# The first group's output products in the half-size scheme of the other groups, and the last store cut in two

## The chip, the cores and the metric

The kernel runs on one core of one Trainium2 chip. The metric is the device time of one execution in microseconds (us), as the median of several runs. Beside these, one execution was taken by the hardware profiler; the durations in the text come from that one.

## The reference

Two stages follow each other. The first is a gated linear recurrence over 768 steps for 4 batches x 8 heads of width 48; the second is a maxout layer on the 3072 resulting tokens of width 384.

```python
f = 1.0 / (1.0 + np.exp(-f_logit))
for t in range(S):                                   # S = 768
    state = f[:, :, t, :, None] * state + np.einsum('bhd,bhe->bhde', k[:, :, t], v[:, :, t])
    y[:, :, t] = np.einsum('bhd,bhde->bhe', q[:, :, t], state)
x = y.transpose(0, 2, 1, 3).reshape(3072, 384)
h = np.maximum(np.maximum(x @ w1, x @ w2), x @ w3)   # w1, w2, w3: 384 x 768
out = h @ w_out                                      # 768 x 384
```

## The kernel before

**Units and groups.** The recurrence is cut into 24 units: a unit is one chunk of 64 steps for two batches, 128 tokens. Four units make a group of 512 tokens, so there are six groups, numbered 0 to 5. As soon as a group's x is complete (xT, feature-major), the group's maxout products are queued, and the units of the next group run between them.

**How the order is set.** Everything is written out by hand in one order (no scheduler moves it), and each engine works through its own part of that order. The products of a group are a Python generator that issues a few matmuls and then yields what they cost; `fill(ns)` draws from it until that many nanoseconds of matmul work are issued. The main loop over units calls `fill` four times in a unit, with the lengths EARLY (units 4 to 7, 2360 ns) or PART (later ones), and issues between these calls the steps of the unit: the block of small matmuls on TensorE (`values`, `sums`, `pairs`, `finish`: lines 415, 433, 396, 504), the scans, transposes and products on VectorE and GpSimd (`scan`, `after`, `before`, `carry`: r L329, ends L339, kh L340, qh L351, state L357), the keys (`keys_by_blocks`, ks L382), and the loads of later units (L183 for f, k, q; L164 for v). SP issues nearly all DMAs, in the written order.

**Maxout without the first weight.** w2 and w3 are kept as differences to w1, so that x @ w1 can leave the maximum and be added at the end: `linear` (L788) computes w1 @ w_out once into w_nat, 18 products of 384 columns, copied out by ScalarE (L792). Then out = hm @ w_out + x @ w_nat, where hm is the maximum of x @ (w2 - w1), x @ (w3 - w1) and 0.

**Group 0** (`ffn_first`) does its products while the weights still arrive and are turned from float64 to fp32. Its outputs (`outputs`, L568) are plain: for each of its four units one bank, nine products of 384 columns (six with hm, three with x), and one copy to o on ScalarE (L572).

**Groups 1 to 5** save matmul work by a scheme of Strassen's kind: seven products of half size replace eight, at the price of sums and differences of the operands. It is used for the inputs (`inputs_by_pairs`, L884, whose weight sums are made by `mix_in`, L853, and whose sums of x are made by `sums_of_x`, L868) and for the outputs (`outputs_by_pairs`, L637, products of 192 columns). For the outputs GpSimd makes the sums of weights (`mix`, L592; `mix_x`, L600) and of hm (`sums_of_hm`, L608: four for each of three pairs of hm rows). Partial results are copied from the banks by ScalarE (L642, L692, L721) and added up by VectorE (L645) and GpSimd (L704) into o. In these groups the first 256 features of x go through the scheme along with hm, as one more pair.

**Rearranged weights.** `place` issues ten small DMAs that copy a weight matrix, with its rows in another order, from one place on the chip to another: w_in[1] to placed[0] and w_in[2] to placed[1] (L458, L465) for the inputs of groups 1 to 5, and w_nat to w_lin for their outputs. placed[2] is then free and holds the sums of `mix_in`; w_in[2] holds those of `mix`; w_in[1] holds the sums of hm.

**The last group** adds its last quarter of the outputs in two halves as the banks c and d are ready (L645), and stores it with one DMA on SP and one on ScalarE's queue (`store_part`, L744), each of 64 partitions x 2 x 192.

Of the kernel before, what the change touches and what calls it, by code (L numbers as in the profile page):

```python
# [9 lines left out]
FP32 = mybir.dt.float32  # L10
# [3 lines left out]
ALU = mybir.AluOpType  # L14
# [32 lines left out]
C = 64  # L47
# [8 lines left out]
def kernel(  # L56
# [12 lines left out]
    nc = tc.nc  # L69
# [8 lines left out]
    GRP = 4  # L78
# [11 lines left out]
    def fast():  # L90
        ctx = ExitStack()
        with ctx:
# [439 lines left out]
            def bank(in_tr=False):  # L532
                if in_tr:
                    return ps_tr.tile([128, TOK], FP32, name="tr")
                return ps_f.tile([128, TOK], FP32, name="p")
# [23 lines left out]
                    t0 = (2 * bp + a) * S + c * C  # L559
                    nc.sync.dma_start(out=out[t0:t0 + C, :], in_=o[a * C:(a + 1) * C, :])  # L560

            def outputs(hm, xT, i):
                p = bank()
                t = slice(i % 2 * UT, (i % 2 + 1) * UT)
                terms = [(hm[:, j, i * UT:(i + 1) * UT], w_out[:, j, :]) for j in range(NJ)]
                terms += [(by_halves(xT)[:, i // 2, k, t], w_nat[:, k, :]) for k in range(NK)]
                for n, (lhsT, rhs) in enumerate(terms):
                    nc.tensor.matmul(p[:, 0:DM], lhsT=lhsT, rhs=rhs, start=(n == 0), stop=(n == NJ + NK - 1))  # L568
                    if n % NK == NK - 1:
                        if n == NJ + NK - 1:  # L570
                            o = o_four[:, i]
                            nc.scalar.copy(o, p[:, 0:DM])  # L572
                            late.append((i, o))
                        yield NK * DM * COLUMN

            HJ, HD = NJ // 2, DM // 2  # L580
            corner = lambda k, n: w_out[:, k::2, n * HD:(n + 1) * HD]
            w_mix = [corner(0, 1)] + [w_in[2][:, :, n * HD:(n + 1) * HD] for n in range(4)]
            x_mix = [w_lin[:, 0, HD:]] + [w_mix[4][:, n] for n in range(2)] + [keep.tile([128, HD], FP32, name="mix")]
            s_mix = [w_in[1][:, n, :].rearrange("q (jj t) -> q jj t", jj=HJ) for n in range(NK)]
            s_last = keep.tile([128, HALF], FP32, name="s_last")
# [1 line left out]

            def mix(n):

                dst, x, y = ((w_mix[2], corner(1, 1), corner(0, 1)), (w_mix[0], corner(0, 1), corner(0, 0)),  # L590
                             (w_mix[1], corner(1, 1), w_mix[0]), (w_mix[3], corner(1, 0), w_mix[1]))[n]
                nc.gpsimd.tensor_tensor(dst, x, y, op=ALU.subtract)  # L592

            def mix_x(n):

# [14 lines left out]
            def sums_of_hm(hm, jj):  # L610
                sums_of_pair(hm[:, 2 * jj], hm[:, 2 * jj + 1], *(t[:, jj] for t in s_mix))
# [7 lines left out]
            def outputs_by_pairs(g, hm, xT):  # L619
                tile_of = lambda p, n: slice((2 * p + n) * UT, (2 * p + n + 1) * UT)  # L620
                half = lambda n: slice(n * HD, (n + 1) * HD)
                order = [*range(HJ - 1), HJ, HJ - 1]
                A = lambda k, n: lambda p: [(xT[:, k] if jj == HJ else hm[:, 2 * jj + k])[:, tile_of(p, n)] for jj in order]
                C = lambda k, n: [(w_lin[:, k] if jj == HJ else w_out[:, 2 * jj + k])[:, half(n)] for jj in order]
                T = lambda i: [x_mix[i] if jj == HJ else w_mix[i][:, jj] for jj in order]
                s1, s2, s4 = (lambda p, t=t, x=x: [(x if jj == HJ else t[:, jj])[:, p * UT:(p + 1) * UT] for jj in order]
                              for t, x in zip(s_mix, s_of_x(xT)))
                X = lambda n: lambda p: [xT[:, 2, tile_of(p, n)]]
                lin, lin_mix = [[w_lin[:, 2, half(n)]] for n in range(2)], [w_mix[4][:, 2]]
                partial = [w_nat[:, n, :] for n in range(NK)]  # L630
                last = g == NU // GRP - 1
                tight = g >= NU // GRP - 2
                begun = set()
# [10 lines left out]
                def add(out, b, n, at=slice(0, 2)):  # L644
                    nc.vector.tensor_tensor(out[:, at], pairs_of(b[:, 0:DM])[:, at], pairs_of(partial[n])[:, at], op=ALU.add)  # L645
# [11 lines left out]
                sums_of_x_pair(xT, 0)  # L657
                into(b, 0, X(0), lin[0])
                yield PLAIN
                into(b, 1, X(0), lin[0])  # L660
# [1 line left out]
                early, rest = slice(len(order) - 1), slice(len(order) - 1, None)  # L662
                for p in range(2):
                    into(a, p, A(0, 0), C(0, 0), early)
                    if p:
# [59 lines left out]
                into(c, 0, s4, C(1, 1))  # L725
                if last:
                    add(o_of(0, 1), c, 1, slice(0, 1))
                yield COST
                into(d, 1, s4, C(1, 1))
                if last:  # L730
                    add(o_of(0, 1), d, 1, slice(1, 2))
                    store_part(g, 0, 1, both)
                else:
                    add(o_of(0, 1), c, 1)
                    late.extend((g * GRP + i, o_four[:, i]) for i in (1, 3, 0, 2))
# [1 line left out]

            o_of = lambda n, c: o_four.rearrange("t (p n) c -> t n p c", p=2)[:, n, :, c * HD:(c + 1) * HD]

            def store_part(g, n, c, queues=one):  # L740

                for a in range(2):
                    t0 = (2 * n + a) * S + 2 * g * C
                    queues[a].dma_start(out=out[t0:t0 + 2 * C, c * HD:(c + 1) * HD].rearrange("(p r) c -> r p c", p=2),  # L744
                                        in_=o_of(n, c)[a * C:(a + 1) * C])

            late = []

# [49 lines left out]
            def ffn_first(xT):  # L798
                hm = new_hm()
                steps = [(j, slice(n * HALF, (n + 1) * HALF)) for n in range(2) for j in range(J_HALF)]  # L800
                steps += [(j, slice(0, TOK)) for j in range(J_HALF, NJ)]
                n_step = 0
                for j, t in steps:
                    w = t.stop - t.start
                    for i in (1, 2):
                        p = yield from product(xT, j, i, t)
                        if i == 1:
                            nc.scalar.copy(hm[:, j, t], p)
                        else:
                            nc.vector.scalar_tensor_tensor(hm[:, j, t], hm[:, j, t], 0.0, p, op0=ALU.max, op1=ALU.max)  # L810
                        round_to(ROUNDED[n_step])
                        load_weights(2, rounded[0] - 1)
                        yield (1 if w == TOK else NK) * w * COLUMN
                        n_step += 1
                        if n_step in TURNED:
                            yield from turn(TURNED[n_step])
                for a in range(NK):
                    if a < 2:
                        for n in range(2 * NK + 2):
                            place(placed[a].bitcast(FP32), w_in[a + 1], n)  # L820
                    for cost in linear(a):
                        round_to(rounded[0] + 1)
                        yield cost
                for n in range(2 * NK + 2):
                    place(w_lin, w_nat, n)
                made = iter([lambda n=n: mix_in(n) for n in range(4)] + [lambda: mix(0)])
                for i in range(GRP):
                    for n, cost in enumerate(outputs(hm, xT, i)):
                        if i or n:
                            next(made, lambda: None)()  # L830
                        if i == GRP - 1 and n == 1:
                            mix(1)
                            if 1 in packed:
                                sums_of_x(1)
                        if i == GRP - 1 and n == 2:
                            for k in range(2, 4):
                                mix(k)
                        yield cost

            w_two = [t.bitcast(FP32) for t in placed[0:2]]
            w_sum = [placed[2].bitcast(FP32)[:, n] for n in range(NK)]

            def mix_in(n):

# [141 lines left out]

            CHECKS = 2 * GRP + 2
            STEP = NK * HALF * COLUMN
            EARLY = 2360
            PART = (33 * TOK + 64 * HD) * COLUMN / (5 * GRP)


# [2 lines left out]
            with tc.manual_schedule():  # L999
# [77 lines left out]
                fill(2 * STEP)  # L1077
                for u in range(GRP, NU):
                    n = u + 1
                    part = EARLY if u < 2 * GRP else PART  # L1080
                    if n == BY_ROWS:
                        scan(n)
                    fill(part)
# [332 lines left out]
```

## Time and profile before

| what | value |
|---|---|
| median of 3 runs | 412.28 us (410.96 to 412.45) |
| the profiled execution | 408.62 us |
| its span, first to last instruction | 406.9 us |
| granted TensorE clock | 0.999 |
| busy: TensorE / VectorE / GpSimd / ScalarE | 391.8 / 293.8 / 246.1 / 180.7 us |
| group 0: `linear` on TensorE, first to last start | 76.2 to 89.8 us |
| group 0: outputs on TensorE, first start to last end | 90.1 to 117.7 us |
| group 1: outputs on TensorE | 152.9 to 177.1 us |
| last matmul's end, last add's end | 401.9, 402.3 us |

How to read the views: a line of the chain or of a timeline has the start, the length, the engine, the line of the kernel, what is done and how often (xN). PE is TensorE, PEld its weight loads, DVE VectorE, ACT ScalarE, POOL GpSimd, SP the engine that issues DMAs (SPq is its queue). An fp32 product of the program stands as two records. A bracket at a line's end is the idle time of the engine before it, and whose end closed it.

### The profile page before, as it was taken

The page shows a single profiled execution, that of the slowest core. Times are in us where ns is not written, and L with a number is a line of the kernel's source. Part 1 is how long each engine was busy: PE and PEld are TensorE (multiplying, and loading weights), DVE is VectorE, ACT ScalarE, POOL GpSimd, SP SyncE. Part 2 cuts the span into 40 slices and gives each one's busy share as a digit, 9 for nine tenths or more (in the row PEclk, how much of TensorE's full clock was granted, in tenths as well). Part 3 has the DMA queues.
Part 4 walks back from the last instruction along what each step waited for, and adds up shares of the span by engine and source line. Part 5 has one row for each costly group of instructions (what it writes and reads, how often), then busy time and mean ns, then how long its engine had stood idle before and what let it go on. Part 6 is the DMA issues. An engine that isn't in the chain of part 4 may idle for free.

```text
span 406.9 us, 11516 instructions
## 1 busy us (share of the span) xinstructions
PE 391.8 (96%) x4598; PEld 331.6 (81%) x4598; DVE 293.8 (72%) x569; ACT 180.7 (44%) x430; POOL 246.1 (60%) x270
## 2 busy tenths in 40 slices
PE   4988999999999999999999999999999999999995
PEld 4766765556678888998889988899988899988994
DVE  6997797997886999897998987998995450012500
ACT  2488787422224541435442344523354425576210
POOL 2189695843888797387486287667477850525700
PEclk9999999999999999999999999999999999999999
DMA  8989986776467776276645367734473003541012
GB/s 173 253 260 280 254 232 92 151 147 89 93 90 111 89 164 129 63 112 86 119 123 100 56 110 92 163 72 81 66 148 107 2 17 98 134 144 59 0 21 63
DMA packets 181562, 47.21 MB, mean 116 GB/s; under 512 B 160448, under 2 KB 179200, under 8 KB 181504
## 3 DMA queue, kind: packets, MB, share of 16 engines
q1 hardware_dynamic: 178032, 45.62, 54.5%
q10 hardware_dynamic: 3472, 0.81, 0.9%
q8 instruction: 37, 0.61, 0.6%
q14 instruction: 21, 0.17, 0.1%
HBM read 37.75 MB, written 4.72 MB: 104 GB/s over the span
## 4 chain that ended last, share of the span: by engine, by line
PE 82%; DVE 8%; issue 2%; SPq 2%; POOL 2%; ACT 1%; DMA 1%; DVEq 0%
PE p L884 16%; PE p L637 15%; PE tr L884 13%; PE tr L637 11%; PE p L542 7%; PE p L568 6%; PE p L788 3%; PE y L415 3%; PE a L396 2%; PE a L433 2%; SPq L183 2%; DVE ks L382 2%; PE y L504 2%; DVE r L329 2%; PE tr L367 1%
## 5 line engine op out<-in xcount | busy, mean ns | idle before, releaser
L382 DVE STREAM_TRANSPOSE ks<-kh 32x128 f32<-32x128 f32 x256 | 77.4, 302 | 10.3 <-POOL kh L340 6.3
L884 PE MATMUL tr<-xT,placed 128*128 128x256 f32 x300 | 71.1, 382 | 0.0
L884 PEld LDWEIGHTS tr<-xT,placed 128*128 128x128 f32 x300 | 56.3, 190 | 8.0
L884 PE MATMUL p<-xT,placed 128*128 128x256 f32 x180 | 44.6, 379 | 0.0
L339 POOL COPY ends<-r 128x8 f32<-128x8 f32 x24 | 6.9, 288 | 56.7 <-DVE r L329 56.7
L340 POOL TENSOR_TENSOR kh<-kt,r 128x512 f32<-128x512 f32 x18 | 32.6, 1810 | 9.5 <-DVE kt L296 9.5
L884 PEld LDWEIGHTS p<-xT,placed 128*128 128x128 f32 x180 | 34.1, 190 | 4.7
L542 PE MATMUL p<-xT,w_in 128*128 128x256 f32 (+1 forms) x108 | 33.9, 458 | 3.1 <-POOL w_in L757 1.9
L329 DVE TENSOR_TENSOR_SCAN r<-gate,from_one 128x520 f32<-128x520 f32 x24 | 32.3, 1345 | 5.9 <-ACT gate L308 2.9
L511 ACT COPY xT<-y 64x256 f32<-64x256 f32 (+1 forms) x60 | 22.1, 369 | 22.6 <-PE y L504 21.8
L347 DVE TENSOR_TENSOR_SCAN prod<-gate,from_inv 128x520 f32<-128x520 f32 x24 | 30.5, 1271 | 0.0
L608 POOL TENSOR_TENSOR w_in<-hm 128x256 f32<-128x256 f32 x15 | 11.1, 740 | 32.0 <-DVE hm L935 29.3
L884 PE MATMUL p<-w_in,placed 128*128 128x256 f32 x120 | 30.4, 382 | 0.0
L645 DVE TENSOR_TENSOR o<-tr,w_in 128x384 f32<-128x384 f32 (+1 forms) x11 | 5.7, 521 | 33.8 <-PE tr L637 29.4
L542 PEld LDWEIGHTS p<-xT,w_in 128*128 128x128 f32 x108 | 19.5, 190 | 12.0 <-issue 6.0
L927 DVE TENSOR_TENSOR hm<-tr,hm 128x512 f32<-128x512 f32 x15 | 10.2, 683 | 22.3 <-PE tr L884 15.4
L258 POOL TENSOR_TENSOR w_in<-top_bits,rest_bits 128x384 uint32<-128x384 uint32 x18 | 21.8, 1218 | 7.2 <-DVE top_bits L252 4.3
L884 PEld LDWEIGHTS p<-w_in,placed 128*128 128x128 f32 x120 | 22.4, 190 | 4.4 <-issue 1.5
L642 ACT COPY w_in<-p 128x384 f32<-128x384 f32 x15 | 7.2, 479 | 41.6 <-PE p L637 41.6
L280 ACT ACTIVATE raw<-top_bits 128x384 f32<-128x384 f32 x48 | 25.2, 526 | 0.4
L637 PE MATMUL p<-w_in,hm 128*128 128x192 f32 x120 | 25.2, 333 | 0.0
L637 PE MATMUL tr<-w_out,w_in 128*128 128x192 f32 x120 | 24.4, 326 | 0.0
(159 smaller groups left out, 913.7 us busy)
## 6 DMA issues: line engine op xcount, KB each, us to landing
raw<-in_moe_w_dram SPq DMA_DIRECT2D x24, 384.0 KB, 4.4
v_ld<-in_v_dram SPq DMA_DIRECT2D x48, 96.0 KB, 3.1
placed<-in_moe_w_dram SPq DMA_DIRECT2D x12, 384.0 KB, 6.1
out_dram<-o SPq DMA_DIRECT2D x46, 96.0 KB, 2.2
placed<-in_moe_w_out_dram SPq DMA_DIRECT2D x6, 384.0 KB, 5.5
f_ld<-in_f_logit_dram SPq DMA_DIRECT2D x36, 64.0 KB, 2.6
k_ld<-in_k_dram SPq DMA_DIRECT2D x36, 64.0 KB, 2.6
q_ld<-in_q_dram SPq DMA_DIRECT2D x36, 64.0 KB, 2.6
```

Source lines behind the costliest of these rows:

```text
L258: nc.gpsimd.tensor_tensor(dst, by(top), by(rest), op=ALU.add)
L280: nc.scalar.activation(over, size, AF.Relu, scale=(-1 / HI_MIN, 1.0)[step - 1], bias=(1.0, -HI_END * (1 - 2.0 ** -24))[step - 1], accum_ou ...
L329: nc.vector.tensor_tensor_scan(r[:, 0:LEN][:, ::-1], flat(gate)[:, ::-1], flat(from_one)[:, ::-1], 1.0, op0=ALU.mult, op1=ALU.max)
L340: (nc.vector if u < BY_ROWS else nc.gpsimd).tensor_tensor(kh.rearrange("p h a t -> p a h t"), kt, by_batch(r[:, 1:LEN + 1].rearrange("p (x ...
L347: nc.vector.tensor_tensor_scan(flat(prod), flat(gate_tiles[u % 2]), flat(from_inv[u % 2]), 1.0, op0=ALU.mult, op1=ALU.max)
L382: nc.vector.transpose(ks[n * 32:(n + 1) * 32, :, par, e0:e0 + 32], kh[p0:p0 + 32, :, a, t0:t0 + 32])
L415: nc.tensor.matmul(y[o:o + DP, a, hp * C:(hp + 1) * C], lhsT=v_ld[s, 2 * hp + par, :], rhs=d["at"][s, par, hp, :], start=(hp == 0), stop=F ...
L511: nc.scalar.copy(xT[o, :, t0 + a * C:t0 + (a + 1) * C], y[i, a, 0:HP * C].rearrange("p (h t) -> p h t", h=HP))
L542: nc.tensor.matmul(p if w < TOK else p.rearrange("p (two t) -> p two t", two=2), lhsT=w_in[i][:, kt, j * 128:(j + 1) * 128], rhs=x[:, t.st ...
L568: nc.tensor.matmul(p[:, 0:DM], lhsT=lhsT, rhs=rhs, start=(n == 0), stop=(n == NJ + NK - 1))
L637: nc.tensor.matmul(b[:, p * HD:(p + 1) * HD], lhsT=x, rhs=w, start=id(b) not in begun, stop=True, skip_group_check=True)
L884: nc.tensor.matmul(b[:, j * HALF:(j + 1) * HALF], lhsT=w[:, (2 * n + j) * 128:(2 * n + j + 1) * 128], rhs=x, start=begin and j == 0, stop= ...
```

## The change

Group 0's outputs are computed by `outputs_by_pairs` too; `outputs` is gone. Since group 0's x isn't in the other row order, only its hm goes through the scheme (three pairs), and x @ w_nat is done plainly, in the four quarters that it appears in (`mixed` is false for group 0). w_nat's columns get one difference of their own (mix(4)). The sums of `mix` now live in placed[2] and those of `mix_in` in w_in[2], so that three of the mixes can be made during `linear`. The copies into placed[1] are issued after `linear`, and with that after the k and q loads of unit 8. The sums of hm of group 0, the `mix_in` and mix(4) are handed out one by one at given yields of the outputs. Units 6 and 7 get a shorter `fill` (LATER). Apart from group 0, the last quarter of the last group's outputs is stored in two parts.

```diff
-            def outputs(hm, xT, i):
...
-                terms = [(hm[:, j, i * UT:(i + 1) * UT], w_out[:, j, :]) for j in range(NJ)]
-                terms += [(by_halves(xT)[:, i // 2, k, t], w_nat[:, k, :]) for k in range(NK)]
...
-            w_mix = [corner(0, 1)] + [w_in[2][:, :, n * HD:(n + 1) * HD] for n in range(4)]
+            spare = placed[2].bitcast(FP32).rearrange("q k c -> q (k c)")
+            w_mix = [corner(0, 1)] + [spare[:, n * NK * HD:(n + 1) * NK * HD].rearrange("q (k c) -> q k c", k=NK)
+                                      for n in range(4)]
...
-                dst, x, y = ((w_mix[2], corner(1, 1), corner(0, 1)), (w_mix[0], corner(0, 1), corner(0, 0)),
-                             (w_mix[1], corner(1, 1), w_mix[0]), (w_mix[3], corner(1, 0), w_mix[1]))[n]
-                nc.gpsimd.tensor_tensor(dst, x, y, op=ALU.subtract)
+                dst, x, y = ((w_mix[2], corner(1, 1), corner(0, 1)), (w_mix[1], w_mix[2], corner(0, 0)),
+                             (w_mix[3], corner(1, 0), w_mix[1]), (w_mix[0], corner(0, 1), corner(0, 0)),
+                             (w_mix[4], w_nat[:, :, 0:HD], w_nat[:, :, HD:]))[n]
+                nc.gpsimd.tensor_tensor(dst, x, y, op=ALU.add if n == 1 else ALU.subtract)
...
             def outputs_by_pairs(g, hm, xT):
...
-                order = [*range(HJ - 1), HJ, HJ - 1]
+                mixed = g > 0
+                order = [*range(HJ - 1), *[HJ] * mixed, HJ - 1]
...
+                else:
+                    X = lambda n: lambda p: [by_halves(xT)[:, p, k, n * UT:(n + 1) * UT] for k in range(NK)]
+                    lin = [[w_nat[:, k, half(n)] for k in range(NK)] for n in range(2)]
+                    lin_mix = [w_mix[4][:, k] for k in range(NK)]
+                    partial = [rests[:, 0], rests[:, 1], rests[:, 0]]
...
                 into(c, 0, s4, C(1, 1))
                 if last:
                     add(o_of(0, 1), c, 1, slice(0, 1))
+                    store_part(g, 0, 1, both, slice(0, 1))
                 yield COST
                 into(d, 1, s4, C(1, 1))
                 if last:
                     add(o_of(0, 1), d, 1, slice(1, 2))
-                    store_part(g, 0, 1, both)
+                    store_part(g, 0, 1, both, slice(1, 2))
...
+                for n in range(2 * NK + 2):
+                    place(placed[0].bitcast(FP32), w_in[1], n)
                 for a in range(NK):
-                    if a < 2:
-                        for n in range(2 * NK + 2):
-                            place(placed[a].bitcast(FP32), w_in[a + 1], n)
-                    for cost in linear(a):
+                    for n, cost in enumerate(linear(a)):
                         round_to(rounded[0] + 1)
+                        if a == 0 and n:
+                            mix(n - 1)
+                        if a == 0 and n == NK - 1:
+                            mix(n)
                         yield cost
-                for n in range(2 * NK + 2):
-                    place(w_lin, w_nat, n)
-                made = iter([lambda n=n: mix_in(n) for n in range(4)] + [lambda: mix(0)])
-                for i in range(GRP):
-                    for n, cost in enumerate(outputs(hm, xT, i)):
...
+                for dst, src in ((placed[1].bitcast(FP32), w_in[2]), (w_lin, w_nat)):
+                    for n in range(2 * NK + 2):
+                        place(dst, src, n)
+                mix(3)
+                made = [[lambda jj=jj: sums_of_hm(hm, jj, slice(0, 2))] for jj in range(HJ)]
+                made[-1] += [lambda jj=jj: sums_of_hm(hm, jj, slice(2, 3)) for jj in range(HJ)]
+                made += [[], [], [], [], [], []]
+                made += [[lambda jj=jj: sums_of_hm(hm, jj, slice(3, 4)) for jj in range(HJ)]]
+                made += [[lambda n=n: mix_in(n)] for n in range(4)] + [[lambda: mix(4)]]
+                made = iter(made)
+                for cost in outputs_by_pairs(0, hm, xT):
+                    for make in next(made, ()):
+                        make()
+                    yield cost
...
-            w_sum = [placed[2].bitcast(FP32)[:, n] for n in range(NK)]
+            w_sum = [w_in[2][:, n] for n in range(NK)]
...
-            EARLY = 2360
+            EARLY, LATER = 2360, 2170
...
-                    part = EARLY if u < 2 * GRP else PART
+                    part = EARLY if u < BY_ROWS else LATER if u < 2 * GRP else PART
```

More of the change, by code (lines that the diff above doesn't have):

```diff
@@ L560, in store @@
                     nc.sync.dma_start(out=out[t0:t0 + C, :], in_=o[a * C:(a + 1) * C, :])
-            def outputs(hm, xT, i):
-                p = bank()
-                t = slice(i % 2 * UT, (i % 2 + 1) * UT)
-                terms = [(hm[:, j, i * UT:(i + 1) * UT], w_out[:, j, :]) for j in range(NJ)]
-                terms += [(by_halves(xT)[:, i // 2, k, t], w_nat[:, k, :]) for k in range(NK)]
[L567 to L574, printed above, removed]
             HJ, HD = NJ // 2, DM // 2
             corner = lambda k, n: w_out[:, k::2, n * HD:(n + 1) * HD]
-            w_mix = [corner(0, 1)] + [w_in[2][:, :, n * HD:(n + 1) * HD] for n in range(4)]
+            spare = placed[2].bitcast(FP32).rearrange("q k c -> q (k c)")
+            w_mix = [corner(0, 1)] + [spare[:, n * NK * HD:(n + 1) * NK * HD].rearrange("q (k c) -> q k c", k=NK)
+                                      for n in range(4)]
             x_mix = [w_lin[:, 0, HD:]] + [w_mix[4][:, n] for n in range(2)] + [keep.tile([128, HD], FP32, name="mix")]
@@ L608, in sums_of_pair, with sums_of_hm @@
                     engine.tensor_tensor(dst, x, y, op=op)
-            def sums_of_hm(hm, jj):
-                sums_of_pair(hm[:, 2 * jj], hm[:, 2 * jj + 1], *(t[:, jj] for t in s_mix))
+            def sums_of_hm(hm, jj, part=slice(0, 4)):
+                sums_of_pair(hm[:, 2 * jj], hm[:, 2 * jj + 1], *(t[:, jj] for t in s_mix), part=part)
             def sums_of_x_pair(xT, n):
@@ L627, in outputs_by_pairs @@
                               for t, x in zip(s_mix, s_of_x(xT)))
-                X = lambda n: lambda p: [xT[:, 2, tile_of(p, n)]]
-                lin, lin_mix = [[w_lin[:, 2, half(n)]] for n in range(2)], [w_mix[4][:, 2]]
-                partial = [w_nat[:, n, :] for n in range(NK)]
+                if mixed:
+                    X = lambda n: lambda p: [xT[:, 2, tile_of(p, n)]]
+                    lin, lin_mix = [[w_lin[:, 2, half(n)]] for n in range(2)], [w_mix[4][:, 2]]
+                    partial = [w_nat[:, n, :] for n in range(NK)]
+                else:
[3 more added lines that the diff above has]
+                    partial = [rests[:, 0], rests[:, 1], rests[:, 0]]
                 last = g == NU // GRP - 1
@@ L656, in outputs_by_pairs @@
                 a, b, c = bank(), bank(True), bank(True)
-                sums_of_x_pair(xT, 0)
+                if mixed:
+                    sums_of_x_pair(xT, 0)
                 into(b, 0, X(0), lin[0])
@@ L664, in outputs_by_pairs @@
                     into(a, p, A(0, 0), C(0, 0), early)
-                    if p:
+                    if mixed and p:
                         sums_of_x_pair(xT, 1)
@@ L738, in fast, with store_part @@
             o_of = lambda n, c: o_four.rearrange("t (p n) c -> t n p c", p=2)[:, n, :, c * HD:(c + 1) * HD]
-            def store_part(g, n, c, queues=one):
+            def store_part(g, n, c, queues=one, p=slice(0, 2)):
                 for a in range(2):
                     t0 = (2 * n + a) * S + 2 * g * C
-                    queues[a].dma_start(out=out[t0:t0 + 2 * C, c * HD:(c + 1) * HD].rearrange("(p r) c -> r p c", p=2),
-                                        in_=o_of(n, c)[a * C:(a + 1) * C])
+                    queues[a].dma_start(
+                        out=out[t0:t0 + 2 * C, c * HD:(c + 1) * HD].rearrange("(p r) c -> r p c", p=2)[:, p],
+                        in_=o_of(n, c)[a * C:(a + 1) * C, p])
             late = []
@@ L823, in ffn_first @@
                         yield cost
-                for n in range(2 * NK + 2):
-                    place(w_lin, w_nat, n)
-                made = iter([lambda n=n: mix_in(n) for n in range(4)] + [lambda: mix(0)])
-                for i in range(GRP):
-                    for n, cost in enumerate(outputs(hm, xT, i)):
[L829 to L838, printed above, removed]
+                for dst, src in ((placed[1].bitcast(FP32), w_in[2]), (w_lin, w_nat)):
+                    for n in range(2 * NK + 2):
+                        place(dst, src, n)
```

## The prediction

> **What bounds the kernel now.** I read the shares by engine first, then the chain of work that ended last.
>
> ```profile
> PE 391.8 (96%) x4598; PEld 331.6 (81%) x4598; DVE 293.8 (72%) x569; ACT 180.7 (44%) x430; POOL 246.1 (60%) x270
> ...
> PE 82%; DVE 8%; issue 2%; SPq 2%; POOL 2%; ACT 1%; DMA 1%; DVEq 0%
> ```
>
> TensorE is busy 96% of the span and carries 82% of the chain: removing matmul time should pay, unless another engine is late next. So I read the chain in order of time around the change (columns: start, us, what), group 0's outputs (L568) being its first lines.
>
> ```profile
> 94.21 11.81 PE p L568 x36
> ...
> 108.03 9.89 PE p L568 x30
> ...
> 127.65 2.95 DMA q_ld<-in_q_dram
> 130.78 0.20 DVE qt L296
> ...
> 157.32 0.69 DVE hm L934
> 158.05 0.59 PE p L637 x2
> ...
> 217.74 3.25 PE tr L637 x20
> ```
>
> After group 0 the chain leaves TensorE. It goes through SP's load queue to the landing of a q load at 130.6, then through VectorE, back to back (with one detour over GpSimd) until 158.0, and only there returns to TensorE. TensorE arrived first and waited 0.41 us for VectorE's hm (L934), the one wait of over 0.3 us that the trace gives its matmuls after 80 us. From 158 it is all TensorE to the end. Next, SP's queue (start, us, what, count), to see what sets that landing.
>
> ```profile
> 84.79 1.27 SPq L458 DMA_DIRECT2D placed<-w_in  x2
> 86.11 5.04 SPq L465 DMA_DIRECT2D placed<-w_in  x8
> 91.20 5.14 SPq L183 DMA_DIRECT2D k_ld<-in_k_dram  x8
> 96.38 4.20 SPq L183 DMA_DIRECT2D q_ld<-in_q_dram  x8
> 100.68 1.22 SPq L458 DMA_DIRECT2D w_in<-w_in  x2
> ...
> 123.88 4.26 SPq L183 DMA_DIRECT2D q_ld<-in_q_dram  x8
> ```
>
> Each line starts where the one before ends: SP issues 68 DMAs from 84.8 to 128.1, 0.64 us each, and waits only 0.6 us in all between 66 and 135. The q load is late because SP is full, not because TensorE is late. Last, GpSimd in the outputs, and the final stores.
>
> ```profile
> 90.25 0.83 POOL L357 TENSOR_TENSOR state<-st,ends 128x384 f32<-128x384 f32 x1
> 92.08 1.82 POOL L853 TENSOR_TENSOR placed<-placed 128x768 f32<-128x768 f32 x1 [1.00 <-DMA placed<-w_in]
> 98.39 0.19 POOL L339 COPY ends<-r 128x8 f32<-128x8 f32 x1 [4.48 <-DVE r L329]
> ...
> 110.86 1.41 POOL L592 TENSOR_TENSOR w_in<-w_out 128x576 f32<-128x576 f32 x1
> ```
>
> ```profile
> 401.96 0.36 DVE L645 TENSOR_TENSOR o<-tr,w_in 128x192 f32<-128x192 f32 x1 [0.87 <-PE tr L637]
> ...
> 402.34 0.60 SPq L744 DMA_DIRECT2D out_dram<-o  x1
> ```
>
> The idle time in brackets on GpSimd is where the new work is laid. The last add ends at 402.3; two 96 KB stores follow (one on SP, one on ScalarE), landing in 2.3 and 2.8 us; the span ends at 406.9.
>
> **What the Trainium skill says.** *GPSIMD Engine Reference*, section 3.1, has a two-input fp32 tensor_tensor of 2048 elements at 4497 ns, 2.2 ns each: an estimate of 1.69 us for 768 elements; the trace has 1.81. Its section 1 says that GpSimd shares its SBUF interface with VectorE's two-input instructions: the trace agrees as far as the same kh (L340) takes 1.18 or 2.02 us. *TensorE: Matmul & The Clock Gate*, "LDWEIGHTS", makes a load columns/1.2, 107 ns; the trace has 190 ns, longer than the 162 ns between matmuls of 192 columns, and yet those run without gaps, so smaller matmuls aren't bound by loads here. *DMA: Bandwidth & Descriptors*, "Anatomy of one DMA", puts about 2.0 us of a DMA into a fixed part, mostly the receipt of the last byte; the 2.1 to 2.8 us of the stores agree, and so halving one can save little.
>
> **The change, part by part.**
>
> Matmuls of group 0's outputs. Removed: 36 of 384 columns, each two records in the trace; 12 records from 98.12 to 101.99 make 0.3225 us each, so 72 x 0.3225 = 23.2 us. Added: 66 of 192 columns, 132 records at 3.25/20 = 0.1625, 21.45 us. Saved: 1.77. Against it: one wait for ScalarE between two uses of a bank (the other five groups show 1.1 us in 5, 0.22 each), and w_nat, which the outputs now need first. Its last part is copied by ScalarE until 90.79, while the two products ahead of it last from 90.11 to 90.76: about 0.15 with the signal. TensorE gains **1.4** if nothing else is late.
>
> GpSimd. Added: twelve sums (L608's 0.72 each, 8.6 us), a fifth mix (1.41) and one o (L704, 1.01). The count of mix and mix_in stays. Three mixes move to 81.6, ahead of ends (L339); they need 4.2 us (5.2 with one op at 2.34) of a gap of 4.73, so kh and qh of that unit come at most 0.5 us late; qh ended at 90.3 and TensorE took it at 93.1. Cost nothing. Then, in order, from 91.1: mix(3) 1.4, six sums 4.3, three 2.1 (98.9); ends, kh, qh, state 4.2 (103.1); three sums 2.1 (105.2); four mix_in 7.2 (112.4); mix(4) 1.4: **113.8**. TensorE comes to the products that read mix(4) after 108 records: 90.1 + 17.6 + two blocks of a unit at 2.0 + 0.4 of new waits + 0.4 of gaps around the blocks (before had that much too) = 112.5. It waits 1.3, and 24 records (3.9) later is done at 117.7; before, it was at 117.73. I take **0.0** as the gain at that point, between 0.8 lower (kh at 1.18 instead of 2.0) and 2 higher (stretched ops). Of the gain, 1.4 goes into a new wait. Behind mix(4) on GpSimd stand o and the next unit's kh and qh; these come to about 118.0, before 118.4 in which TensorE would take qh at the earliest (120.43 before, less 2.0): no further wait.
>
> SP. 16 k and q loads of unit 8 go ahead of the 10 copies into placed[1]; the sum of issues ahead of the q load that lands at 130.6 is the same 68, so I leave it there, plus or minus 1.0 (two issues in the stretch took 1.28 and 1.67 instead of 0.49, and may fall elsewhere). VectorE's waits for the earlier q and k (1.9 and 0.5 at 98 to 103) go, but behind it waits TensorE's next block (1.15 us idle at 121) and the later q load (2.74 idle to 130.78): worth nothing. placed[1], issued until about 100.4 and landing in up to 4, is there when mix_in starts at 105.2 (mix_in now writes w_in[2], which those copies read: the same wait). The sums overwrite w_in[1], whose copies were issued by 78.2: landed long before 92.5.
>
> VectorE gets two adds of 0.557, ScalarE one copy more of 0.48: both sit in idle time (2.74 before 130.78; 2 to 5 us between copies). Groups 1 to 5 keep their order; the lower part (LATER) only keeps the units where they stood in it: 16 parts lose 8 x 0.19 = 1.5 us, about what the outputs lose.
>
> What is late next, even if mix(4) were early: VectorE's chain from 130.78 to 158.0 doesn't hang on group 0. TensorE, earlier by any amount, waits at L934 that much longer than 0.41. So the matmul part brings **0** at 158 unless the q load lands earlier.
>
> The last quarter of outputs. c's half goes out at 401.1, 1.2 us before the rest, on both queues (0.6 to 0.7 an issue, over before 402.3); 2 x 48 KB remain. From 2.8, the slower landing of the two, to the 2.2 of an undisturbed store: **0.4**, between 0.1 and 0.6.
>
> Sum: 408.62 (the profiled execution, span 406.9) - 0.4 = 408.2. The median shown is 412.28, 3.7 above it; where the others spend that isn't shown, and I carry the difference: **411.9**.
>
> **Rivals.** (a) The saving comes through: 1.4, with the 0.41 of L934 and 0.4 of the stores, 2.2 us, 410.1. It needs GpSimd's list faster by 1.3 and the q load earlier by 1.8. For it: the unprofiled runs are 2.3 to 3.8 us longer than the profile, so their lateness may lie elsewhere. Against: two independent bounds. (b) Slower: mix(4) comes later than 114.2 (0.4 more than estimated), from which L934's 0.41 no longer absorbs it. Three of the ops stretched by VectorE as kh is, 0.8 each, make it 116.2: 2.0 later than that, less 0.4: 413.9; placed[1] landing after 105.2 does the same. For it: VectorE is busy 17 of 20 us there. (c) The reordered loads move the q load 1 us later: +1.0 - 0.4, 412.9; 1 us earlier alone brings 0.4 more, since mix(4) holds TensorE. (d) It does what it says and nothing is seen: stores included, 412.3.
>
> **How the numbers follow.** Likeliest case with (c) and (d) 0.60, all within 0.5% (2.1 us, about what a measurement of this kernel can tell from no change). (a) 0.22, of it 0.14 beyond 0.5%, because its 2.2 lies on that edge and could reach 2.6. (b) 0.18, of it 0.10 beyond. Faster 0.14, same 0.76, slower 0.10. The likeliest case alone spans 411.3 to 412.9; the range leaves out the far ends of (a) and (b): 409.8 to 413.4.
>
> **What would show it.** Right: a wait of TensorE of about 1.3 us for GpSimd at the products of w_mix[4] with the last x of group 0; group 0's outputs ending about 117.7; a q load landing near 130.6 and TensorE waiting for hm around 158; the last landing 0.4 sooner. Wrong: no such waits and the records after 158 earlier by over 1 us (a), or a GpSimd wait over 2 us (b).

## The result, and the profile after

The changed kernel is slower. Its runs have a median of 413.6 us (412.81 to 415.31, 14 runs); the kernel before, run beside it, has 410.08 us. The ratio is 1.0084, with a 95% interval of 1.0058 to 1.011. The forecast was 411.9, a ratio of 0.999 to its 412.28, with a range up to 413.4: direction and range were both missed. In us it looks nearer than it was: the three runs of the kernel before on which it was built had the median 412.28, all fourteen have 410.08. What happened is the mechanism of rival (b), at a higher price.

The profiled execution took 414.71 us, its span 413.0 against 406.9 before. First the shares and the clock of TensorE on the page of the changed kernel:

```profile
PE 392.8 (95%) x4658; PEld 341.9 (83%) x4658; DVE 296.5 (72%) x571; ACT 181.3 (44%) x431; POOL 257.5 (62%) x284
...
PEclk9999999999969999999999999999999999999999
...
PE 79%; SPq 7%; POOL 5%; DMA 2%; DVE 2%; issue 2%; ACT 2%; POOLq 0%
```

TensorE should have lost 1.8 us of work; its busy time rose by 1.0. In one slice of the 40 (around 119 us) its granted clock was near 0.6, where the page of before has none under 0.9. In the chain, GpSimd went from 2% to 5%. TensorE's waits say where (waiting engine, line, releaser, then total, times, longest):

```profile
PE p L629 <- POOL placed L577: 4.2, 1, 4.2
...
PE p L629 <- POOL kh L340: 0.7, 1, 0.7
```

L577 is `mix` in the changed kernel (L592 before), L629 the products of the outputs, L593 the sums of hm, L850 `mix_in`, L634 the ScalarE copy. The 4.2 us are the wait for mix(4). The timeline of TensorE around it:

```profile
112.95 2.11 PE L629 MATMUL p<-placed,hm 128*128 128x192 f32 x12
119.26 4.21 PE L629 MATMUL p<-placed,xT 128*128 128x192 f32 x12 [4.20 <-POOL placed L577]
123.26 2.46 PE L629 MATMUL tr<-w_out,w_in 128*128 128x192 f32 x12
125.56 1.03 PE L881 MATMUL p<-xT,placed 128*128 128x256 f32 x4
```

The last line is where group 1 starts. In the profile of before it starts here:

```profile
117.73 1.03 PE L884 MATMUL p<-xT,placed 128*128 128x256 f32 x4
```

Read the starts. From 119.26 to 123.26 twelve records took 4.00 us, then twelve 2.30; at the usual 0.1625 each they take 1.95. So 2.4 us more went after the wait had ended. In the table by stretches each line has the stretch, its length, the busy times of PE, PEld, DVE, ACT and POOL, and then the granted clock of TensorE:

```profile
100.00:120.00 20.00, 15.14 (x204) 14.27 (x203) 15.80 (x30) 3.41 (x9) 19.92 (x16) 0.93 0.54 106
120.00:140.00 20.00, 20.00 (x208) 18.02 (x208) 13.96 (x33) 6.95 (x14) 13.42 (x16) 0.90 0.70 104
```

The fifth busy time is GpSimd's: 19.92 of 20 us. It had become the bound of that stretch. Its timeline (start, us):

```profile
88.92 0.19 POOL L339 COPY ends<-r 128x8 f32<-128x8 f32 x1 [1.16 <-DVE r L329]
...
92.88 0.84 POOL L357 TENSOR_TENSOR state<-st,ends 128x384 f32<-128x384 f32 x1
...
99.53 3.03 POOL L593 TENSOR_TENSOR hm<-hm 128x256 f32<-128x256 f32 x3
...
110.63 1.82 POOL L850 TENSOR_TENSOR w_in<-w_in,placed 128x768 f32<-128x768 f32 x1
112.41 2.75 POOL L850 TENSOR_TENSOR placed<-placed,placed 128x768 f32<-128x768 f32 x1
115.12 2.73 POOL L850 TENSOR_TENSOR w_in<-placed,w_in 128x768 f32<-128x768 f32 x1
117.82 1.39 POOL L577 TENSOR_TENSOR placed<-w_in 128x576 f32<-128x576 f32 x1
```

and, beside it, VectorE's:

```profile
86.74 2.12 DVE L329 TENSOR_TENSOR_SCAN r<-gate,from_one 128x520 f32<-128x520 f32 x1
...
98.87 1.80 DVE L329 TENSOR_TENSOR_SCAN r<-gate,from_one 128x520 f32<-128x520 f32 x1
...
111.86 1.69 DVE L329 TENSOR_TENSOR_SCAN r<-gate,from_one 128x520 f32<-128x520 f32 x1
...
114.29 1.96 DVE L347 TENSOR_TENSOR_SCAN prod<-gate,from_inv 128x520 f32<-128x520 f32 x1
```

Each stretched instruction of GpSimd (three sums in 3.03 instead of 2.1, two mix_in of 2.75 and 2.73 instead of 1.82) starts while one of VectorE's scans runs, and the scans are stretched too: 1.69 to 2.12 us for r. In the profile of before the first r of these took 1.24; the third was stretched there already, beside a mix_in and a mix of GpSimd:

```profile
84.99 1.24 DVE L329 TENSOR_TENSOR_SCAN r<-gate,from_one 128x520 f32<-128x520 f32 x1
...
110.89 2.48 DVE L329 TENSOR_TENSOR_SCAN r<-gate,from_one 128x520 f32<-128x520 f32 x1
```

This execution's start-up, to the first product of `linear`, was 1.74 us longer (77.93 instead of 76.19; the eleven variants e1 to e11 described below lie between), so times are compared from that product:

| from `linear`'s first product, us | before | after | e1 | e2 | e3 | e5 | e6 | e7 | e8 |
|---|---|---|---|---|---|---|---|---|---|
| group 1 starts (group 0's outputs are done) | 41.54 | 47.63 | 40.87 | 41.54 | 45.61 | 40.86 | 40.87 | 40.76 | 41.54 |
| SP begins to issue unit 10's q load | 47.69 | 48.77 | 47.95 | 49.36 | 49.30 | 48.48 | 38.62 | 40.73 | 39.90 |
| the last add ends | 326.13 | 331.27 | 326.59 | 327.89 | 329.25 | 327.09 | 324.50 | 324.38 | 325.17 |

The span's 6.1 us more are 1.74 of start-up, 5.14 up to the last add, and 0.78 less after it (3.80 instead of 4.58).

### The profile page after: what moved, and what is told of

It reads as the page before. It is cut to its first block, busy times and chain, and to the rows that moved or that the text cites. A ratio compares the mean times of both kernels' runs of the same rounds, so it can differ in the third digit from the quotient of the medians.

```text
span 413.0 us, 11671 instructions
## 1 busy us (share of the span) xinstructions
PE 392.8 (95%) x4658; PEld 341.9 (83%) x4658; DVE 296.5 (72%) x571; ACT 181.3 (44%) x431; POOL 257.5 (62%) x284
## 4 chain that ended last, share of the span: by engine, by line
PE 79%; SPq 7%; POOL 5%; DMA 2%; DVE 2%; issue 2%; ACT 2%; POOLq 0%
PE p L881 19%; PE p L629 16%; PE tr L881 15%; PE tr L629 12%; PE p L542 6%; PE y L415 3%; SPq L183 3%; PE a L396 2%; SPq L174 2%; PE y L504 2%; PE a L433 2%; DMA raw<-in_moe_w_dram 2%; POOL w_in L850 1%; SPq L164 1%; POOL w_in L752 1%
## 5 line engine op out<-in xcount | busy, mean ns | idle before, releaser
L881 PE MATMUL tr<-xT,placed 128*128 128x256 f32 x180 | 44.4, 384 | 0.0
L329 DVE TENSOR_TENSOR_SCAN r<-gate,from_one 128x520 f32<-128x520 f32 x24 | 33.2, 1384 | 6.4 <-issue 3.0
L881 PEld LDWEIGHTS tr<-xT,placed 128*128 128x128 f32 x180 | 33.5, 190 | 4.9
L593 POOL TENSOR_TENSOR w_in<-hm 128x256 f32<-128x256 f32 x18 | 13.3, 739 | 33.5 <-DVE hm L932 33.5
L347 DVE TENSOR_TENSOR_SCAN prod<-gate,from_inv 128x520 f32<-128x520 f32 x24 | 31.6, 1317 | 0.0
L881 PE MATMUL tr<-xT,w_in 128*128 128x256 f32 x120 | 30.8, 379 | 0.0
L629 PE MATMUL p<-placed,hm 128*128 128x192 f32 x144 | 29.8, 333 | 0.7 <-POOL kh L340 0.7
L881 PE MATMUL p<-xT,placed 128*128 128x256 f32 x120 | 29.2, 379 | 0.0
L629 PE MATMUL tr<-w_out,w_in 128*128 128x192 f32 x144 | 29.0, 329 | 0.0
L629 PEld LDWEIGHTS p<-placed,hm 128*128 128x128 f32 x144 | 23.8, 190 | 2.3 <-ACT w_in L634 1.1
L899 POOL TENSOR_TENSOR hm<-hm,rest_bits 128x512 f32<-128x512 f32 x15 | 19.1, 1272 | 10.2 <-ACT hm L889 10.2
```

Of the source, the lines that this page charges most:

```text
L329: nc.vector.tensor_tensor_scan(r[:, 0:LEN][:, ::-1], flat(gate)[:, ::-1], flat(from_one)[:, ::-1], 1.0, op0=ALU.mult, op1=ALU.max)
L347: nc.vector.tensor_tensor_scan(flat(prod), flat(gate_tiles[u % 2]), flat(from_inv[u % 2]), 1.0, op0=ALU.mult, op1=ALU.max)
L629: nc.tensor.matmul(b[:, p * HD:(p + 1) * HD], lhsT=x, rhs=w, start=id(b) not in begun, stop=True, skip_group_check=True)
L881: nc.tensor.matmul(b[:, j * HALF:(j + 1) * HALF], lhsT=w[:, (2 * n + j) * 128:(2 * n + j + 1) * 128], rhs=x, start=begin and j == 0, stop= ...
L899: nc.gpsimd.tensor_tensor(out(n, 0), out(n, 0), first, op=ALU.add)
```

## The experiments

All but m1 are edits of the changed kernel or, where said, of the kernel before. Ratios are to the kernel before, run on the same chip, with 95% intervals.

**e1: mix(4) ahead of the four mix_in.**

```diff
-                made += [[lambda n=n: mix_in(n)] for n in range(4)] + [[lambda: mix(4)]]
+                made += [[lambda: mix(4)]] + [[lambda n=n: mix_in(n)] for n in range(4)]
```

> The changed kernel with one edit: mix(4) is made ahead of the four mix_in instead of behind them. Theory A (the loss is mix(4) standing last in GpSimd's list, so that TensorE idles 4.2 us and then runs 2.4 us of products at a lowered clock): both go; group 0's outputs end about 0.5 us earlier than in the kernel before (counted from the start of linear), no wait of TensorE for GpSimd over 0.5 us; total 0.8 to 1.5 us faster than before, about 6 faster than the change. Theory B (GpSimd, or the copies into placed[1], are late as a whole): the wait only moves to group 1, whose first products of w_sum then wait 2 us or more, and the total stays 2 us or more above before.

Measured: 410.05 us, ratio 1.0003 (0.9987 to 1.0019). Moving one 1.4 us instruction takes the whole loss back, but the expected gain of 0.8 to 1.5 us is not there. TensorE's waits of e1 no longer have the 4.2 us but two others behind it, in unit 9's block:

```profile
PE a L396 <- POOL qh L351: 0.9, 1, 0.9
PE y L504 <- ACT seen L422: 0.8, 1, 0.8
```

GpSimd is now busy with mix_in until 117.5 and gives qh at 120.9; VectorE, which had to wait 5.06 us for kh, does its next add only at 121.1; ScalarE's copy into the buffer that this add reads starts at 121.75, when the add (until 121.64) and GpSimd's state (until 121.69, which the trace names) have just ended, and seen stands behind that copy. From `linear` to group 1 TensorE is 0.67 us ahead of before; these two waits take it back, and the last add ends 0.46 us later than before. The profiled execution was the fastest of e1's 22 (408.37 us), so the other runs may lose elsewhere.

**e2: the store in two parts alone** (`store_part` and its two calls put into the kernel before).

> The kernel before with only the last quarter of the outputs stored in two parts. The profile of the change has 3.8 us from the last add to the end of the span against 4.6 before: if that is the stores, this is 0.8 us faster than before. As forecast: 0.4. Rival: the fixed part of a store is all that counts, 0.

Measured: 409.89 us, ratio 0.9995 (0.9976 to 1.0015): 0.2 us less, plus or minus 0.8, so the times tell neither 0.8 nor 0.4 from nothing. In the ten profiles with the split store the end came 3.76 to 3.82 us after the last add six times, and 4.62 to 4.99 four times; in the three without, 4.58 to 4.60 each time. The means, 4.22 and 4.59, differ by the forecast 0.4, but no single execution shows it: it is 0.8 or nothing. What decides between the two is not shown.

**e3: the wait filled with products that nothing reads.**

```diff
+                if g == 0:
+                    busy(11)
                 into(a, 0, X(1), lin_mix)
```

> The changed kernel with 11 matmuls of 256 columns into a spare bank (22 records, 4.7 us, results unused) ahead of the products that read mix(4), so that TensorE is busy while it would wait. Theory A1 (the idle time lowers the granted clock): the 12 records of these products take 1.95 us instead of 4.0 and the next 12 take 1.95 instead of 2.3, and the total falls by about 2 us against the change (2.4 less what the filling overruns the wait). Rival A2 (the products are slow because of what they read): they stay at 4.0 us and the total rises by up to 0.5.

The timeline of TensorE, at the same place:

```profile
113.53 4.91 PE L985 MATMUL p<-from_one,ident 128*128 128x256 f32 x22
118.28 2.11 PE L629 MATMUL p<-placed,xT 128*128 128x192 f32 x12
120.22 2.11 PE L629 MATMUL tr<-w_out,w_in 128*128 128x192 f32 x12
```

The same 24 records start 1.94 and 1.95 us apart. GpSimd is no faster, and yet group 1 starts 2.02 us earlier than in the changed kernel. So the idle time itself lowers the clock of what follows. In the runs the gain is smaller, 412.49 us (ratio 1.0065, 1.0037 to 1.0092), an interval that overlaps the changed kernel's: the times alone do not show this point. The mean granted clock, which was taken in every run, agrees with the trace: on average 0.993 over the 14 runs of the changed kernel (0.989 to 0.996), 0.997 over the 8 of e3, and 0.998 over the 47 of the kernel before beside them. The Trainium skill describes it (*TensorE: Matmul & The Clock Gate*, Part 1: after an idle window of about 3.4 us the array runs at half its clock until it has been active for about as long). The traces agree on the half: 4.00 us for 1.95, and a granted clock of 0.50 (118 to 123 us in the changed kernel). On the times they agree only roughly: in the changed kernel the clock fell 2.1 us after TensorE's last product and stayed low for 6.8 us, in e9 (below) it fell after 3.7 us and stayed low for 3.4. Waits of up to 1.3 us between other products left the clock alone.

**m1: the two engines' instructions beside each other,** in a kernel of its own, whose output is zeros: six GpSimd additions of 128x768, alone and beside four kinds of VectorE instruction.

> Not the kernel: a measurement by itself, the outputs are zeros. GpSimd adds two fp32 tiles of 768 columns six times in each of five stretches while VectorE does nothing, scans of 520, transposes of 32x128, sums of two SBUF tiles of 512, sums of a bank and an SBUF tile of 512. Theory C (VectorE's instructions with two SBUF inputs hold GpSimd up): 1.8 us alone, beside the transposes and the sums with a bank; 2.5 us or more beside the scans and beside the sums of two SBUF tiles, and these themselves take longer than alone. Rival: 1.8 in all five, the stretched instructions of the change had another cause.

The timeline, GpSimd's six additions together: alone, beside scans, beside 32x128 transposes, beside additions with two SBUF inputs, beside additions with one input in a bank:

```profile
6.67 11.19 POOL L107 TENSOR_TENSOR z<-x,y 128x768 f32<-128x768 f32 x6 [0.43 <-DVE f L101]
...
18.30 16.25 POOL L107 TENSOR_TENSOR z<-x,y 128x768 f32<-128x768 f32 x6
...
39.88 11.19 POOL L107 TENSOR_TENSOR z<-x,y 128x768 f32<-128x768 f32 x6 [0.16 <-DVE f L101]
...
52.32 13.24 POOL L107 TENSOR_TENSOR z<-x,y 128x768 f32<-128x768 f32 x6
...
74.60 11.23 POOL L107 TENSOR_TENSOR z<-x,y 128x768 f32<-128x768 f32 x6
```

And the scans, by their source line (shortest, median and longest, in ns):

```profile
L88 DVE TENSOR_TENSOR_SCAN s<-f,g x10: 1241/2655/2659, 18.3 to 38.2; 128x520 f32<-128x520 f32 x10
```

One GpSimd addition beside scans, and beside VectorE's additions with two SBUF inputs, and then these additions themselves (the same three values):

```profile
L107 POOL TENSOR_TENSOR z<-x,y x6: 2612/2614/2787, 18.3 to 31.9; 128x768 f32<-128x768 f32 x6
...
L107 POOL TENSOR_TENSOR z<-x,y x6: 2129/2131/2200, 52.3 to 63.4; 128x768 f32<-128x768 f32 x6
...
L94 DVE TENSOR_TENSOR h<-f,g x18: 691/691/2177, 52.2 to 73.4; 128x512 f32<-128x512 f32 x18
```

Transposes and bank additions cost GpSimd nothing; scans cost it 0.84 us an addition and are themselves stretched from 1.24 to 2.66. So the rival, 1.8 us in all five stretches, is out. That is the contention which the Trainium skill names (*GPSIMD Engine Reference*, section 1: for VectorE instructions with two SBUF inputs, which a scan is). Another page (*SBUF — State Buffer*, on the shared port pair) calls it an exclusive lock under which the loser fully blocks. Here six additions beside scans took 16.25 us, 2.71 for an addition and a scan, less than the 1.80 + 1.24 = 3.04 of one after the other, so part of them still overlapped.

**e4: the ten copies into placed[1] back inside `linear`,** ahead of the k and q loads of unit 8.

> The changed kernel with the ten copies into placed[1] issued inside linear again, as in the kernel before, and so ahead of the k and q loads of unit 8. Theory A (GpSimd's list is too long for the place of mix(4); placed[1] was there in time): the wait for mix(4) stays at 3.5 to 5 us and the time stays within 0.3% of the changed kernel's 413.6. Theory B (mix_in and with it mix(4) are late because the copies land late): the mix_in start at once, the wait shrinks by 1 us or more, and the time falls by 1 to 3 us.

Measured: 415.63 us, ratio 1.014 (1.0085 to 1.0195), and the wait for mix(4) was 5.1 us. The copies were not what made mix(4) late: in the changed kernel the chain leads from mix(4) back to their landing at 105.1 us, but GpSimd had no gap there, and with the copies issued earlier mix(4) came no sooner. But the time rose by 0.5%, more than the expected 0.3%. With them back, the q load of unit 8 came later, qh waited 1.17 us for it on GpSimd, and everything behind qh with it; group 1 starts 1.2 us later than in the changed kernel (48.80 us from `linear`). This part of the change helps.

**e5: e1, with the last two mix_in behind the next unit's kh, qh and state.**

```diff
-                made += [[lambda: mix(4)]] + [[lambda n=n: mix_in(n)] for n in range(4)]
+                made += [[lambda: mix(4)]] + [[lambda n=n: mix_in(n)] for n in range(2)]
+                made += [[], [], [], [], [], []]
+                made += [[lambda n=n: mix_in(n)] for n in range(2, 4)]
```

> The changed kernel with mix(4) ahead of the four mix_in, as in the run e1_mix4_first, and moreover the last two mix_in only after the next unit's kh, qh and state. Theory A (TensorE's later waits in e1 for qh, 0.9 us, and for seen, 0.8 us, come from mix_in standing ahead of kh and qh on GpSimd): both waits go, group 0's outputs with unit 9's block end 1.5 to 2.5 us earlier from the start of linear than in e1, and then TensorE waits 0.7 to 2 us for hm at about 157 because VectorE's chain from the q load doesn't move; in sum 0.3 to 1.5 us less than the kernel before, 408.5 to 409.8 where that is 410.1. Rival: the last two mix_in now hold up the weight sums or the sums of x that group 1 needs, the wait moves there in full, and the time stays within 0.3 us of the kernel before.

Measured: 410.32 us, ratio 0.9993 (0.9965 to 1.0022), its runs spread from 406.94 to 411.42: no gain, where 0.3 to 1.5 us was expected. In unit 9's block both waits of e1 are gone, as expected; but then TensorE's timeline has

```profile
152.71 0.67 PE L504 MATMUL y<-qh,state 48*48 48x64 f32 x32 [1.14 <-ACT seen L422]
...
160.54 1.19 PE L629 MATMUL p<-w_out,hm 128*128 128x192 f32 x4 [0.69 <-DVE hm L933]
```

that is, unit 11's block and the hm of group 1, both behind VectorE. What was gained came back as waits 30 us later.

**e6: e5, with the ten copies into w_lin issued after unit 10's k and q loads.**

```diff
-                for dst, src in ((placed[1].bitcast(FP32), w_in[2]), (w_lin, w_nat)):
+                for dst, src in ((placed[1].bitcast(FP32), w_in[2]),):
...
                     if BY_ROWS < u + 2 < NU and u % GRP == 0:
                         load(u + 2, one, "q")
+                    if u == 2 * GRP:
+                        for i in range(2 * NK + 2):
+                            place(w_lin, w_nat, i)
```

> As e5, and the ten copies into w_lin are issued by SP after the k and q loads of unit 10 instead of ahead of them, so that the q load which landed at 130 to 134 us lands about 6 us earlier. Theory A (the prediction's step that VectorE's chain from the q load to hm at 158 is late next once TensorE is ahead): TensorE's wait for hm at about 157 goes, and the time is 0.7 to 2 us less than in e5. Rival: that chain is late for other work of VectorE, the wait stays, and e6 equals e5 within 0.4 us.

Measured: 407.12 us, ratio 0.9926 (0.9901 to 0.9951), its runs within 406.28 and 407.92. In SP's queue the q load that began at 126.21 us in e5 now stands as

```profile
115.50 4.15 SPq L183 DMA_DIRECT2D q_ld<-in_q_dram  x8
```

and TensorE has neither wait. VectorE's chain from the q load was the next bound. It was worth 3.2 us, more than the 2 expected at most.

**e7: e6, with group 0's products of x moved behind others,** those with the first half of w_nat behind the first products of hm, those with the second half ahead of bank a's later use.

> As e6, and in group 0 the six products of x with the first half of w_nat go behind the next products of hm, and those with the second half ahead of bank a's second use, so that the wait for w_nat (0.27 us) and for ScalarE's copy of bank a (0.8 us) are covered by other matmuls. If these two waits still cost what the trace shows, e7 is 0.6 to 1.1 us below e6 and 1.5 to 3.5 us below the kernel before. Rival: TensorE only arrives earlier at a later wait (hm or seen), and e7 equals e6 within 0.3 us.

Measured: 406.89 us, ratio 0.9928 (0.9903 to 0.9952), the same as e6. The two waits went, and TensorE's list has another in their place:

```profile
PE p L629 <- ACT rest_bits L634: 0.6, 1, 0.6
```

Group 1 starts only 0.1 us earlier: a bank's copy was waited for at another product.

**e8: the kernel before with e6's order of the copies alone.**

> The kernel before with one edit: the ten copies into w_lin are issued by SP after the k and q loads of unit 10 instead of ahead of them. Nothing of the change is in it. Theory A (TensorE's wait for VectorE's chain in the kernel before is only the 0.41 us at hm, so that the early q load is worth little by itself and the rest of e6's gain is group 0's scheme): 0 to 0.6 us less than the kernel before, and e6 below it by 1.2 to 2.6 us. Rival (the unprofiled runs of the kernel before lose more to that chain than its profile shows, and e6's gain is all of it the q load's): e8 equals e6 within 0.4 us.

Measured: 408.22 us, ratio 0.9953 (0.9935 to 0.9971). More than expected: 2.1 us, where the profile of before showed 0.41; and e6 is 1.1 us below it, so each theory has a part. The spread shrank too: 407.87 to 409.13 in 14 runs, while the kernel before had 407.93 to 412.04 in 18, fourteen of these from 409.43 up. What such a run looks like, e2's profile shows: an execution of 410.08 us of the kernel before with the store alone changed. TensorE's waits there have

```profile
PE y L504 <- ACT seen L422: 1.3, 1, 1.3
...
PE p L637 <- DVE hm L936: 0.7, 1, 0.7
```

at 152.5 and 160.3 us, the two places of e5. Its q load was issued 1.67 us later than in the profile of before (49.36 and 47.69 in the table), although SP's order is the same, and its last add ends 1.76 us later. So most runs of the kernel before lose to the q load's chain, 1 to 4 us by the times, and its profiled execution was one of those that hardly did. Why the same order takes SP longer in one execution than in another is not shown.

**e9: the changed kernel with e6's order of the copies alone.**

> The changed kernel with the ten copies into w_lin issued after the k and q loads of unit 10, and nothing else: mix(4) stays behind the four mix_in. Theory A (in the changed kernel the bound is GpSimd's list, and the q load's chain has 4 us of room behind the wait for mix(4)): within 0.3% of the changed kernel, ratio to the kernel before 1.005 to 1.012, and the wait for mix(4) stays at about 4 us. Rival (part of the changed kernel's loss in the unprofiled runs is the q load, as it is in the kernel before): 1 to 2 us less than the changed kernel, ratio 0.999 to 1.004.

Measured: 413.36 us, ratio 1.0081 (1.0054 to 1.0109), the changed kernel's within 0.3 us. Its wait for mix(4) stayed:

```profile
PE p L629 <- POOL placed L577: 4.2, 1, 4.2
```

With TensorE 5 us late, the q load has room. The slow clock behind the same wait cost less in this execution, 1.5 us instead of 2.4: twelve records in 3.47 us, and the next twelve in 1.95.

```profile
118.43 3.64 PE L629 MATMUL p<-placed,xT 128*128 128x192 f32 x12 [4.18 <-POOL placed L577]
121.90 2.11 PE L629 MATMUL tr<-w_out,w_in 128*128 128x192 f32 x12
123.85 1.03 PE L881 MATMUL p<-xT,placed 128*128 128x256 f32 x4
```

**e10 and e11: e6 and e8 once more, beside each other.**

> The kernel of e6_q_load_early once more, on the same chip as the next one, to see what group 0's scheme is worth where neither GpSimd's list nor the q load holds it up: 1.0 to 1.6 us less than the next one by the sum of the matmuls (1.77 less 0.27 and 0.8 of new waits would be 0.7; the profiles to the last add give 0.8 to 1.1); rival: nothing, within 0.3 us, if an engine other than TensorE is the bound by then.

> The kernel of e8_q_load_early_alone once more, beside the one above. About 0.4 to 0.5% below the kernel before, and 0.7 to 1.6 us above e10 if the scheme pays; equal to it within 0.3 us if not.

Measured: 406.84 (ratio 0.9922, 0.9892 to 0.9953) and 408.62 us (ratio 0.9966, 0.9951 to 0.9982). Group 0's outputs in the scheme, with the split store, are worth 1.8 us here and 1.1 between e6 and e8, once neither GpSimd's list nor the q load takes it back. The sum of the matmuls leaves 0.7, and the store's mean 0.4 makes that 1.1. The 1.8 is above this and above the expected 1.0 to 1.6; what makes up the rest is not shown. e6 is the version to keep.

## Why the prediction was wrong, by its own steps

**TensorE's saving: right in kind, half the size.** Forecast 1.4. From `linear` to group 1, e1, e5 and e6 are 0.67 us ahead of before. The 1.77 of matmul time is there. The term that was off is the wait for a bank: 0.22, taken from the other groups, against 0.8 here (0.66 in the trace and the gaps around it). The wait stands in the list under kh, which ended at 104.79, just before these products start at 104.82; but by the program they read nothing of kh. They write bank a, which ScalarE copies out first (L634, 104.20 to 104.68), and in e7, with other products laid between, the wait is gone. This is read from the program and the times; no run separates the copy from kh. In groups 1 to 3 of the kernel before a unit's block lies between the two uses of the bank. w_nat cost 0.27 instead of 0.15.

**GpSimd's list: the step that failed.** Forecast end of mix(4) 113.8; measured 119.21, which is 117.47 on the clock of before: 3.67 late. Its terms: the state ahead of mix(3) was 0.88 later, because the three moved mixes, which "cost nothing", stretched VectorE's scan r to 2.12 us, and ends had to wait 1.16 for it; the three sums laid before ends took 0.93 longer; the four mix_in 9.1 instead of 7.2. These three make up the 3.7. Each is the same oversight. The idle times of GpSimd in the profile of before end with "<-DVE r L329", that is, when VectorE's scan ends; so the scan lies in their last 1.24 us, work laid there runs beside it, and m1 gives the price. The forecast took durations from rows that had run alone, and kept the stretched ones for the range. Since the gaps were chosen by that releaser, stretched ones had to be the middle of the estimate.

**TensorE's wait, and what was left out.** TensorE came 0.8 later than the forecast 112.5, so the wait was 1.3 + 3.67 - 0.8 = 4.2, as in the list. Then came a term that the prediction did not have, left at nothing without a reason: the idle time lowered the clock, 2.4 us more. The forecast had group 1 start where it did before; 3.67 and 2.4 make it 6.07 later, and 6.09 was measured (47.63 less 41.54). This is rival (b), given 0.18. Its example put mix(4) at 116.2 and the loss against no change at 1.6 us; with 117.5, and the clock, the runs show 3.5.

**"No further wait" behind mix(4): wrong.** It cannot be seen in the changed kernel, where TensorE is late anyway; e1 shows it, 0.9 for qh and 0.8 for seen. It follows from the same list: qh ended at 120.90, 2.8 us after the forecast 118.0 on the clock of before.

**What is late next: right, and undervalued.** That a TensorE which comes earlier only waits for VectorE's chain from the q load is what e5 and e6 show: the same 410 us with the late load, 407 with the early one. But 0.41 us was its price in one execution, a favourable one; in e2's it was 1.25 and 0.69. By e8 and e11 the kernel before loses 2.1 and 1.3 us there in its median run. This also closes the sum. The changed kernel, which does not lose it (e9 equals it), is 5.1 us behind by the profile, and e9 is 4.7 behind e11; but it is only 3.5 behind the median of the kernel before, which does lose it. The 3.7 us between the profile and the median, which the prediction carried along unexplained, were a hint of it.

**SP's order: nearly right, and idle.** The q load began 1.1 us later than before (48.77 less 47.69), just outside the plus or minus 1.0. It cost nothing there, and the new order need not be the cause: in e2, with the old order, it began 1.67 later.

**The store: not decided.** 0.4 forecast, 0.2 plus or minus 0.8 measured; the profiles give 0.4 as a mean of 0.8 and nothing. The section that the prediction cites for the fixed part of a DMA describes DMAs that GpSimd issues; these stores are issued by SP and ScalarE.

## What to carry to other kernels

Before work is laid into an engine's idle time, read what ended that time: if it is a scan of VectorE, price GpSimd's work at the stretched rate, and add what the stretch does to the scan. An instruction on which TensorE waits goes ahead of those that are wanted only later (e1 got back the whole loss by moving one line), and a wait of 4 us or more is priced with the slow clock behind it, 1.5 to 2.4 us here. One profile shows one execution: where its time lies at the lower end of the runs, a wait of 0.4 us in it may be 2 in the median, as it was here.

## What the runs showed of the hardware that was not expected

A wait of TensorE of 4.2 us cost another 2.4 us after it in one execution (12 records in 4.00 instead of 1.95 us, the next 12 in 2.30) and 1.5 in another; one of 5.1 us (e4) cost 2.4. Products that nothing reads, laid into the wait, kept the clock at full speed. A GpSimd addition of 128x768 beside a scan takes 2.61 instead of 1.80 us and makes the scan 2.66 instead of 1.24; beside a VectorE addition with two SBUF inputs it takes 2.13 (and that addition up to 2.18 instead of 0.69); beside transposes or additions from a bank 1.80 and 1.81.
